# Loads of the first three tiles moved together ahead of the weights, and two fills moved from GpSimd to ScalarE, in an RWKV and two-expert-layer kernel

## The chip, the cores and the metric

The kernel runs on one core of a Trainium2 chip. The metric is the device time of one execution in microseconds (us): before the change 930.45 us is the median of three runs (929.73 to 933.15).

## The reference

Three layers follow one another. The first is a linear attention with a decaying state, for 4 batches, 8 heads, 768 steps and a head size of 48; its output, taken as 3072 tokens of 384 values, goes through a gated feed-forward layer (384 to 1536 and back), and this through a layer of eight experts in which each token goes to the expert with the largest logit.

```python
for t in range(S):                                   # attention, per batch and head
    cur = np.einsum('bhd,bhe->bhde', u[None] * kt, vt)
    y[:, :, t] = np.einsum('bhd,bhde->bhe', rt, state + cur)
    state = wt[:, :, :, None] * state + np.einsum('bhd,bhe->bhde', kt, vt)
xn = x / sqrt(mean(x * x) + 1e-6) * rms_g            # gated layer
x = (silu(xn @ w_gate) * (xn @ w_val)) @ w_out
e = argmax(x @ w_gate2)                              # experts, for each token
out = prob(e) * sigmoid(x @ w_output_gate)[e] * (relu(x @ w1[e]) @ w2[e])
```

The weights of the gated layer arrive as 64-bit floats; the others are 32-bit.

## The kernel before

**Tiles.** A tile is 128 steps of one batch; there are 24, numbered so that tiles 0 to 3 are the first 128 steps of the four batches. The gated layer works on blocks of three tiles; block 0 is tiles 0 to 2. While TensorE works on a block, the attention of the next block is laid in slots between its matmuls.

**Loads of a tile.** All go through the queue of SyncE (SP), which issues in program order. `load_tile` (L296) brings the transposed decays, k and r (the "set": two loads of 96 KB at L310 and two of 192 KB at L312, 576 KB together, into 48 of each 64 partitions), `load_rk` (L314) r and k with tokens on partitions (384 KB, L318, one buffer for all tiles) and `load_v` (L320) v (192 KB, L325). The padding rows of a set are filled by `pads` (L278): four fills and one of five columns; tile 2 has a set of its own in the ring, whose pads are on GpSimd (POOL, L303). Tiles 0 and 1 have theirs filled by VectorE and GpSimd.

**Weights of the gated layer.** They come in 18 pieces of 768 KB. Pieces 0, 1, 3 and 4 are the gate and value columns of one 128-wide slice f (two loads of 384 KB each), pieces 2 and 5 are rows of `w_out` for two slices (one load). `decode` (L101) turns the 64-bit words into two 32-bit parts in five stages: the loads; L113 on ScalarE and L114 on VectorE; L118 on VectorE and L122 on GpSimd; L125 on ScalarE; L130 on VectorE or GpSimd. One `decode_step` (L680) issues the loads of the piece two further on and takes earlier pieces on by a stage each.

**Attention of a tile** (`attention`, L339) is a generator with nine steps: (1) scan of the decays on VectorE, L357, and on GpSimd the products r*k*u, L363 and L364; (2) L367 and L368; (3) second scan L373, product L376, the loads of a later set, the sum over r*k*u on VectorE, L380, the loads of the next r and k, and L384 on GpSimd; (4) transposes and their copy, L391 and L393; (5) matmuls L403 and masks L407; (6) matmuls L420, sum L424, then on ScalarE and GpSimd the norm, L428 to L430; (7) matmuls L435, state copies L445, load of a later v; (8) L449; (9) transposes L453 and the two parts of x, L457 and L458.

**Start.** Before the first block the steps of tiles 0 to 2 are issued in the order of the tuple `START_SEQ` (L42): 0, 1 or 2 is the next step of that tile, 9 is a decode step, and a negative number is that many idle matmuls that warm TensorE (L332). Each engine runs its instructions in the order in which they are issued here. The first matmul of the gated layer (L165) needs x of tiles 0 to 2 and the first piece.

The loads in the order in which SP issues them: set 0, r and k of 0, v of 0, piece 0, set 1, piece 1, v of 1, piece 2, set 2, v of 2; then from the steps: set 3, r and k of 1, set 4, r and k of 2, v of 3, piece 3, r and k of 3, v of 4, pieces 4 and 5. `rk` has one buffer, so r and k of tile 1 are issued after L380 of tile 0, and those of tile 2 after L380 of tile 1:

```python
        nc.vector.tensor_reduce(g, rku, axis=AX.X, op=ALU.add)   # L380
        load_rk(i + 1)                                           # L381
```

The ring has 12 slots of 1536 words per partition and six larger ones; its first users are `kts`, two spare buffers, `turned` and v of tile 2, and then the decoded weights go round it. `states` (128x1536) is zeroed by GpSimd at L707.

Of the kernel before, what the change touches and what calls it, by code (L numbers as in the profile page):

```python
# [9 lines left out]
F32 = mybir.dt.float32  # L10
# [4 lines left out]
AF = mybir.ActivationFunctionType  # L15
# [7 lines left out]
def kernel(  # L23
# [15 lines left out]
    ROUTE_AT=(0, 1),  # L39
    OFFS=((0, 0, 6.7, 7.5, 8.8, 10.5, 11.4, 11.5, 12.7), (0, 1.6, 3.2, 4.8, 6.4, 8, 9.6, 11.6, 13.8)),  # L40
    TGAP=(8.9, 9.0),
    START_SEQ=(-11, 0, 0, 0, -4, -4, -6, -4, 0, 9, 1, 0, 1, -4, 0, 1, 1, 2, -4, 0, 0, 1, 9, 2, 0, 1, -4, 2, -6, 1, 9, 2, 1, 2, -4, 1, 2, 9, -2, 2, 2, 9, -6, 2, 9),  # L42
):
    nc = tc.nc
    B, S, _, H, D = rkv.shape
    N, DM = out.shape
    DFF = w_gate.shape[1]
    E, _, F2 = w1.shape
    P = 128
# [19 lines left out]
    SEG = P + 1  # L69
    FLAT = NPR * SEG  # L70
    KR = 2 * NPR * P
    SETW = KR + FLAT + 1
# [13 lines left out]
    def slot_of(n, dtype, name, big=None):  # L86

        if big is None:
            big = taken[0] % 3 == 2
            taken[0] += 1  # L90
        size = WSLOT if big else SLOT
        t = ring.tile([P, size], dtype, tag="big" if big else "ring", bufs=6 if big else 12, name=name)
        return t[:, 0:n]
# [75 lines left out]
    def ring_view(shape, dtype=F32, big=None):  # L169
        n = 1  # L170
        for x in shape:
            n *= x
        t = slot_of(n, dtype, "rv", big)
        names = "abc"[:len(shape)]
        dims = " ".join(names)
        return t.rearrange(f"p ({dims}) -> p {dims}", **dict(zip(names[1:], shape[1:])))
# [90 lines left out]
    p1 = ph1.enter_context(tc.tile_pool(name="p1", bufs=1))  # L267
# [8 lines left out]
    states = p1.tile([P, B, NPR, 2 * D], F32, name="states")  # L276

    def pads(t, engs):  # L278

        for q in range(2):  # L280
            engs[q].memset(t[64 * q + 32:64 * q + 64, KR:SETW], 1.0)
        for q in range(2):
            engs[q].memset(t[64 * q + 32:64 * q + 64, 0:KR], 0.0)
        engs[1].memset(t[:, KR:SETW:SEG], 0.0)

    def parts(t):

        kr = t[:, 0:KR].rearrange("p (x a t) -> p x a t", x=2, a=NPR)
        return kr, t[:, KR:SETW]

    tiles = [(b, ch) for ch in range(NCH) for b in range(B)]
    vt = {}
    rk = {}
    sets = {}

    def load_tile(i):  # L296

        if i >= len(tiles):
            return
        b, ch = tiles[i]  # L300
        if i == NSET:
            t = ring_view([SETW], big=True)
            pads(t, (nc.gpsimd, nc.gpsimd))  # L303
        else:
            t = sets_w[(i - (i > NSET)) % NSET]
        sets[i] = t
        kr, w = parts(t)
        w = w[:, 1:SETW - KR].rearrange("p (a t) -> p a t", t=SEG)[:, :, 0:P]
        for q in range(2):
            nc.sync.dma_start(out=w[64 * q:64 * q + D], in_=feat[b, ch, q, :, 0])  # L310
        for q in range(2):
            nc.sync.dma_start(out=kr[64 * q:64 * q + D], in_=feat[b, ch, q, :, 1:3])  # L312

    def load_rk(i):  # L314
        if i < len(tiles):
            b, ch = tiles[i]
            rk[i] = p1.tile([P, 2, H, D], F32, tag="rk", name="rk")
            nc.sync.dma_start(out=rk[i], in_=rkv[b, ch * P:ch * P + P, 0:2])  # L318

    def load_v(i):  # L320
        if i >= len(tiles):
            return
        b, ch = tiles[i]
        t = ring_view([H, D], big=False) if i == 2 else p3.tile([P, H, D], F32, tag="v", bufs=2, name="vt")
        nc.sync.dma_start(out=t, in_=rkv[b, ch * P:ch * P + P, 2])  # L325
        vt[i] = t
# [9 lines left out]

    START = START_SEQ

    def attention(c, i, xh, xl, col):  # L339
# [37 lines left out]
        if i != NSET:  # L377
            load_tile(i + NSET + (i < NSET))
        g = p2.tile([P, H], F32, tag="g", name="g")
        nc.vector.tensor_reduce(g, rku, axis=AX.X, op=ALU.add)  # L380
        load_rk(i + 1)  # L381
        vv = vt.pop(i)
        y = p2.tile([P, H, D], F32, tag="y", name="y")
# [235 lines left out]
    with tc.manual_schedule():  # L619
        one_b = const.tile([P, P], BF16, name="one_b")  # L620
        nc.vector.memset(one_b, 1.0)
        pads(sets_w[0], (nc.vector, nc.gpsimd))
        load_tile(0)
        c = constants()
        load_rk(0)
        load_v(0)
        pads(sets_w[1], (nc.vector, nc.gpsimd))
        kts = ring_view([NSET + 1, NPR * P], big=False).rearrange("p i (a t) -> p i a t", a=NPR)
        pieces = []
        for f in range(KF):  # L630
# [38 lines left out]
        def advance(m, stage):  # L669
            if m < len(pieces):  # L670
                while len(gens_w) <= m:
                    m0 = len(gens_w)
                    gens_w.append([decode(m0, *pieces[m0][:2], m0 % 3 == 2, *pieces[m0][2:]), 0])
                while gens_w[m][1] < stage:
                    next(gens_w[m][0])
                    gens_w[m][1] += 1
# [21 lines left out]

        turned = ring_view([4, KD * P], big=False)
        advance(0, 1)  # L700
        load_tile(1)
        advance(1, 1)
        load_v(1)
        advance(2, 1)
        load_tile(2)
        load_v(2)
        nc.gpsimd.memset(states, 0.0)  # L707

        xs = new_x(0)
        first = [attention(c, a, xs[0], xs[1], a * P) for a in range(sizes[0])]  # L710
# [32 lines left out]
        for j in range(NB):  # L743
# [24 lines left out]
            for f in range(KF + 2):  # L768
# [9 lines left out]
                if j == NB - 1:  # L778
                    if f >= 3:
                        next(xw, None)  # L780
                    if f == KF - 3:
                        xg0 = ring_view([EARLY // P, ROW])
                        nc.sync.dma_start(
                            out=xg0, in_=scr[0:EARLY, :].rearrange("(t p) c -> p t c", p=P)
# [253 lines left out]
        for ui, (k, r0, n) in enumerate(units):  # L1038
# [4 lines left out]
            a, b2 = ew[k]  # L1043
# [24 lines left out]
            for f in range(KF2 + 2):  # L1068
                if f < KF2:
                    o = bank("a", 2, [P, n])  # L1070
                    t = a[f // 2]
# [18 lines left out]
                if f >= 2:  # L1090
                    g = f - 2
                    hh, hl = hs.pop(g)
                    t = b2[g // 2]
# [36 lines left out]
        for q in ("w1", "w2"):  # L1130
            ov[q] = []
            for _ in range(2):
                t = slot_of(1536, F32, "ov")
# [57 lines left out]
```

## Time and profile before

| | before |
|---|---|
| median of three runs | 930.45 us (929.73 to 933.15) |
| the profiled execution | 934.85 us |
| its span, first to last instruction | 933.1 us |
| mean granted TensorE clock | 0.962 of full speed |
| busy: TensorE (PE) | 876.9 us, 94% |
| busy: VectorE (DVE) | 533.7 us, 57% |
| busy: ScalarE (ACT) | 314.8 us, 34% |
| busy: GpSimd (POOL) | 227.9 us, 24% |
| SP's load queue | 79.67 MB, 29.2% of 16 DMA engines' time |

The profile is one execution of the program. Its stretches differ: the start (attention of three tiles and the first decode steps), block 0 beside the rest of the decoding, and then blocks 1 to 7 and the experts, in which TensorE is hardly idle. Engines are named as in the profile: PE, DVE, ACT, POOL, and SPq for SP's queue. An idle time in brackets stands ahead of an instruction, with what ended it.

### The profile page before, as it was taken

The numbers are of one execution on the slowest core, as the hardware profiler recorded it, in microseconds if no ns is written. First come the engines' busy times: TensorE is split into PE (matmuls) and PEld (weight loads), VectorE is DVE, ScalarE is ACT, GpSimd is POOL, SyncE is SP. The second block draws the span as 40 slices with busy tenths as digits, with TensorE's granted clock in tenths as the row PEclk, the third lists the DMA queues.
The fourth block names the chain that finished last, engine by engine and source line by source line (L and its number), as shares of the span: only waits on it lengthen the run. The fifth ranks groups of instructions, "written<-read, shape, count | busy, mean of one in ns | idle before, by whom it ended". The sixth has DMA issues, their size and how long they took to land. (4 is left out here: it accounts for less than half of the span.)

```text
span 933.1 us, 14620 instructions
## 1 busy us (share of the span) xinstructions
PE 876.9 (94%) x5543; PEld 846.7 (91%) x5543; DVE 533.7 (57%) x1073; ACT 314.8 (34%) x654; POOL 227.9 (24%) x298
## 2 busy tenths in 40 slices
PE   6568779999999999999999999999899999999995
PEld 4458769999999999999999999999899999999994
DVE  5589785656565376366456465434537565556551
ACT  1254433322322323323222322323334344434430
POOL 6465552212231131132123113010010100122111
PEclk7679899999999999999999999999999999999997
DMA  9564252274131023022122122001143453554510
GB/s 229 129 218 131 90 161 50 83 213 137 46 110 51 9 86 82 13 78 56 47 69 60 52 68 78 1 27 51 52 146 98 151 179 107 159 163 152 174 47 21
DMA packets 65300, 90.40 MB, mean 97 GB/s; under 512 B 6259, under 2 KB 56035, under 8 KB 65229
## 3 DMA queue, kind: packets, MB, share of 16 engines
q1 hardware_dynamic: 60973, 79.67, 29.2%
q0 software_dynamic: 3568, 9.57, 2.8%
q8 instruction: 44, 0.72, 0.3%
q10 hardware_dynamic: 688, 0.22, 0.1%
q14 instruction: 27, 0.22, 0.1%
HBM read 73.22 MB, written 16.73 MB: 96 GB/s over the span
## 5 line engine op out<-in xcount | busy, mean ns | idle before, releaser
L165 PE MATMUL a<-xh,gv 128*128 128x384 f32 x1152 | 324.1, 347 | 0.0
L165 PEld LDWEIGHTS a<-xh,gv 128*128 128x128 f32 x1152 | 213.7, 191 | 2.2
L165 PE MATMUL a<-xl,gv 128*128 128x384 f32 x576 | 195.9, 340 | 0.0
L500 DVE TENSOR_TENSOR sil<-a,sil 128x384 f32<-128x384 f32 x96 | 53.2, 554 | 110.6 <-PE a L165 110.2
L165 PE MATMUL a<-xh,w1s 128*128 128x256 f32 (+7 forms) x432 | 111.9, 325 | 1.4 <-DVE hl L876 1.1
L165 PEld LDWEIGHTS a<-xl,gv 128*128 128x128 f32 x576 | 110.3, 192 | 0.0
L502 ACT ACTIVATE hh<-sil 128x384 fp32r<-128x384 f32 x96 | 50.3, 524 | 162.2 <-DVE sil L500 162.2
L514 PE MATMUL l<-wo,hh 128*128 128x400 f32 x288 | 102.2, 355 | 0.0
L498 ACT ACTIVATE sil<-a 128x384 f32<-128x384 f32 x96 | 47.2, 492 | 156.7 <-PE a L165 151.6
L515 PE MATMUL l<-wo,hh 128*128 128x400 f32 x288 | 99.8, 347 | 0.0
L516 PE MATMUL l<-wo,hl 128*128 128x400 f32 x288 | 99.2, 345 | 0.0
L244 POOL DMA_INDIRECT out_dram<-row,iu x30 | 34.9, 1165 | 208.5 <-DVE row L887 188.7
L876 DVE SCALAR_TENSOR_TENSOR hl<-a,hh 128x256 fp32r<-128x256 f32 (+7 forms) x80 | 40.7, 510 | 74.3 <-ACT hh L875 74.3
L165 PEld LDWEIGHTS a<-xh,w1s 128*128 128x128 f32 x432 | 76.7, 188 | 2.8 <-DVE hl L876 1.6
L505 DVE TENSOR_TENSOR hl<-sil,hh 128x384 fp32r<-128x384 f32 x96 | 56.2, 585 | 34.9 <-ACT hh L502 34.9
L875 ACT ACTIVATE hh<-a 128x256 fp32r<-128x256 f32 (+7 forms) x80 | 36.5, 456 | 101.9 <-PE a L165 100.2
L165 PE MATMUL a<-xl,w1s 128*128 128x256 f32 (+7 forms) x216 | 69.7, 323 | 0.1
L384 POOL TENSOR_TENSOR y<-vt,g 128x384 f32<-128x384 f32 x23 | 22.0, 958 | 169.2 <-issue 62.6
L165 PE MATMUL l<-rows,hh 128*128 128x384 f32 (+3 forms) x240 | 63.0, 344 | 0.0
L420 PE MATMUL m<-vt,am 128*128 128x48 f32 x368 | 55.1, 278 | 4.5 <-DVE am L407 4.5
L420 PEld LDWEIGHTS m<-vt,am 128*128 128x128 f32 x368 | 51.2, 204 | 5.5 <-DVE am L407 5.4
L514 PEld LDWEIGHTS l<-wo,hh 128*128 128x128 f32 x288 | 54.9, 190 | 0.1
(216 smaller groups left out, 1510.8 us busy)
## 6 DMA issues: line engine op xcount, KB each, us to landing
raw<-in_moe_w_dram SPq DMA_DIRECT2D x64, 384.0 KB, 3.3
rk<-in_rkv_dram SPq DMA_DIRECT2D x24, 384.0 KB, 4.2
set<-in_feat_dram SPq DMA_DIRECT2D x46, 192.0 KB, 3.9
scr<-zrow SPq DMA_DIRECT2D x8, 788.0 KB, 7.6
set<-in_feat_dram SPq DMA_DIRECT2D x46, 96.0 KB, 3.0
vt<-in_rkv_dram SPq DMA_DIRECT2D x23, 192.0 KB, 2.5
raw<-in_moe_w_gate_dram SPq DMA_DIRECT2D x8, 384.0 KB, 4.0
raw<-in_moe_w_val_dram SPq DMA_DIRECT2D x8, 384.0 KB, 3.9
```

The lines of the kernel that those rows point to most:

```text
L165: nc.tensor.matmul(o, a, b, start=start and i == 0, stop=stop and i == 2, skip_group_check=True)
L244: ins = nc.gpsimd.indirect_dma_start(out=dst, out_offset=bass.IndirectOffsetOnAxis(ap=idx, axis=0), in_=rows, in_offset=None, bounds_check ...
L420: nc.tensor.matmul(yp[:, 2 * p + q], am[q][:, p], vv[:, 2 * p + q], start=not ch, stop=True, skip_group_check=True,)
L498: nc.scalar.activation(out=sil, in_=o, func=AF.Silu)
L500: nc.vector.tensor_tensor(out=sil, in0=pg[1], in1=sil, op=ALU.mult)
L502: nc.scalar.activation(out=hh, in_=sil, func=AF.Copy)
L505: nc.vector.tensor_tensor(out=hl, in0=sil, in1=hh.bitcast(F32), op=ALU.subtract)
L514: nc.tensor.matmul(o, hh[:, sl], wh, start=f == 0, stop=False)
L515: nc.tensor.matmul(o, hh[:, sl], wl, start=False, stop=False)
L516: nc.tensor.matmul(o, hl[:, sl], wh, start=False, stop=f == KF - 1)
L875: nc.scalar.activation(out=hh, in_=o, func=AF.Relu)
L876: nc.vector.scalar_tensor_tensor(out=hl, in0=o, scalar=0.0, in1=hh.bitcast(F32), op0=ALU.max, op1=ALU.subtract)
```

## The change

The tuple moves one decode step (9) behind three steps of tiles 0 and 1 and four idle matmuls. Set 1, r and k of tile 1 and v of tile 1 are loaded ahead of piece 0, and set 2, r and k of tile 2 and v of tile 2 ahead of pieces 1 and 2. r and k of tiles 1 and 2 get a slot of the ring of their own (2 x 768 words). The four large fills of tile 2's pads, and that of `states`, are done by ScalarE, as an activation that copies a column of ones times 1 or 0. The fill of the five columns of tile 1's and tile 2's pads, and of tile 0's, is on GpSimd, as it was.

```diff
-    START_SEQ=(-11, 0, 0, 0, -4, -4, -6, -4, 0, 9, 1, 0, 1, -4, 0, 1, 1, 2, -4, 0, 0, 1, 9, 2, 0, 1, -4, 2, -6, 1, 9, 2, 1, 2, -4, 1, 2, 9, -2, 2, 2, 9, -6, 2, 9),
+    START_SEQ=(-11, 0, 0, 0, -4, -4, -6, -4, 0, 1, 0, 1, -4, 9, 0, 1, 1, 2, -4, 0, 0, 1, 9, 2, 0, 1, -4, 2, -6, 1, 9, 2, 1, 2, -4, 1, 2, 9, -2, 2, 2, 9, -6, 2, 9),
...
     def pads(t, engs):
-        for q in range(2):
-            engs[q].memset(t[64 * q + 32:64 * q + 64, KR:SETW], 1.0)
-        for q in range(2):
-            engs[q].memset(t[64 * q + 32:64 * q + 64, 0:KR], 0.0)
-        engs[1].memset(t[:, KR:SETW:SEG], 0.0)
+        for a, x in ((slice(KR, SETW), 1.0), (slice(0, KR), 0.0)):
+            for q in range(2):
+                rows = slice(64 * q + 32, 64 * q + 64)
+                if engs[q] is nc.scalar:
+                    nc.scalar.activation(
+                        out=t[rows, a], in_=one_b[rows, 0:1].to_broadcast([32, a.stop - a.start]),
+                        func=AF.Copy, scale=x,
+                    )
+                else:
+                    engs[q].memset(t[rows, a], x)
+        nc.gpsimd.memset(t[:, KR:SETW:SEG], 0.0)
...
             t = ring_view([SETW], big=True)
-            pads(t, (nc.gpsimd, nc.gpsimd))
+            pads(t, (nc.scalar, nc.scalar))
...
     def load_rk(i):
-        if i < len(tiles):
+        if i < len(tiles) and i not in sets_rk:
             b, ch = tiles[i]
-            rk[i] = p1.tile([P, 2, H, D], F32, tag="rk", name="rk")
+            sets_rk.add(i)
+            if i in (1, 2):
+                rk[i] = more_rk[:, i - 1].rearrange("p (x h d) -> p x h d", x=2, h=H)
+            else:
+                rk[i] = p1.tile([P, 2, H, D], F32, tag="rk", name="rk")
             nc.sync.dma_start(out=rk[i], in_=rkv[b, ch * P:ch * P + P, 0:2])
...
         pads(sets_w[1], (nc.vector, nc.gpsimd))
+        load_tile(1)
+        more_rk = ring_view([2, 2 * DM], big=False)
+        load_rk(1)
+        load_v(1)
         kts = ring_view([NSET + 1, NPR * P], big=False).rearrange("p i (a t) -> p i a t", a=NPR)
...
         advance(0, 1)
-        load_tile(1)
+        load_tile(2)
+        load_rk(2)
+        load_v(2)
         advance(1, 1)
-        load_v(1)
         advance(2, 1)
-        load_tile(2)
-        load_v(2)
-        nc.gpsimd.memset(states, 0.0)
+        flat = states.rearrange("p b a d -> p (b a d)")
+        nc.scalar.activation(
+            out=flat, in_=one_b[:, 0:1].to_broadcast(flat.shape), func=AF.Copy, scale=0.0
+        )
```

## Rows read from the trace of the kernel before

**Rows 1.** Stretches: us, then busy us (instructions) of each engine, clock, DMA share, GB/s.

```profile
3.00:9.50 6.50, 6.01 (x28) 2.87 (x26) 3.94 (x6) 0.55 (x1) 6.03 (x15) 1.00 0.96 254
9.50:14.40 4.90, 2.64 (x23) 1.37 (x20) 1.83 (x3) 0.60 (x1) 4.09 (x5) 0.77 1.11 228
14.40:18.80 4.40, 1.00 (x4) 0.91 (x5) 4.30 (x7) 0.91 (x1) 2.63 (x1) 0.50 1.08 337
...
23.30:31.40 8.10, 3.31 (x26) 2.94 (x24) 0.81 (x2) 0.12 (x1) 0.00 (x0) 0.71 0.90 193
31.40:62.70 31.30, 19.30 (x117) 15.41 (x118) 25.39 (x41) 15.13 (x30) 20.84 (x17) 0.72 0.51 166
62.70:150.00 87.30, 71.30 (x421) 67.72 (x422) 73.98 (x97) 41.01 (x79) 45.75 (x30) 0.88 0.38 119
150.00:900.00 750.00, 745.41 (x4783) 729.52 (x4782) 412.95 (x897) 250.69 (x532) 141.51 (x216) 1.00 0.30 89
```

**Rows 2.** Timeline of DVE in the start: start, us, instruction, idle before.

```profile
14.46 0.56 DVE L114 TENSOR_SCALAR dt<-raw 128x768 uint32<-128x768 uint32 x1 [1.03 <-DMA raw<-in_moe_w_val_dram]
...
33.51 0.55 DVE L380 TENSOR_REDUCE g<-rk 128x8 f32<-128x384 f32 x1 [9.36 <-POOL rk L364]
...
37.06 0.55 DVE L114 TENSOR_SCALAR dt<-rv 128x768 uint32<-128x768 uint32 x1
37.64 1.64 DVE L118 SCALAR_TENSOR_TENSOR dt<-rv,dt 128x768 uint32<-128x768 uint32 x1
...
47.47 0.94 DVE L118 SCALAR_TENSOR_TENSOR dt<-raw,dt 128x768 uint32<-128x768 uint32 x1
...
61.30 1.00 DVE L114 TENSOR_SCALAR dt<-rv 128x768 uint32<-128x768 uint32 x1
62.22 0.95 DVE L130 TENSOR_TENSOR gv<-dt,gv 128x768 fp32r<-128x768 f32 x1
```

**Rows 3.** Timeline of POOL in the start.

```profile
7.40 1.93 POOL L283 MEMSET rv<- 32x1024 f32 x2
...
9.43 1.39 POOL L707 MEMSET states<- 128x1536 f32 x1
10.77 1.00 POOL L363 TENSOR_TENSOR rk<-rk 128x384 f32<-128x384 f32 x1
...
16.15 2.63 POOL L122 TENSOR_TENSOR dt<-dt,raw 128x768 int32<-128x768 int32 x1 [1.81 <-DVE dt L118]
31.42 0.99 POOL L363 TENSOR_TENSOR rk<-rk 128x384 f32<-128x384 f32 x1 [12.63 <-DMA rk<-in_rkv_dram]
```

**Rows 4.** Timeline of SP's queue in the start: when a load was issued.

```profile
6.34 1.08 SPq L310 DMA_DIRECT2D set<-in_feat_dram  x2
...
24.33 0.35 SPq L318 DMA_DIRECT2D rk<-in_rkv_dram  x1
...
26.90 0.84 SPq L312 DMA_DIRECT2D set<-in_feat_dram  x2
34.09 0.35 SPq L318 DMA_DIRECT2D rk<-in_rkv_dram  x1
...
47.21 0.48 SPq L109 DMA_DIRECT2D rv<-in_moe_w_out_dram  x1
```

**Rows 5.** Waits of SP's queue, 0 to 60 us: total us, times, longest.

```profile
SPq L318 <- DVE g L380: 10.8, 2, 8.1
...
SPq L109 <- DMA raw<-in_moe_w_val_dram: 2.2, 1, 2.2
```

**Rows 6.** Single loads: r and k of tile 1, and piece 5, with us to landing.

```profile
rk<-in_rkv_dram SPq DMA_DIRECT2D x1, 384.0 KB, 7.0
...
rv<-in_moe_w_out_dram SPq DMA_DIRECT2D x1, 768.0 KB, 8.3
```

**Rows 7.** Timeline of ACT in the start.

```profile
9.76 0.60 ACT L393 ACTIVATE rv<-m 128x512 f32<-128x512 f32 x1 [6.21 <-PE m L391]
...
35.75 0.83 ACT L125 ACTIVATE gv<-dt 128x768 fp32r<-128x768 f32 x1
```

More of the change, by code (lines that the diff above doesn't have):

```diff
@@ L293 @@
     rk = {}
+    sets_rk = set()
     sets = {}
```

## The prediction, made before the changed kernel was timed

> **What bounds the kernel now.** I read the table of stretches first. From 150 to 900 us PE is busy for 745 of 750 us at full clock, so what starts earlier there ends earlier by as much; the change can only move what lies ahead. Ahead of it are a start of 62.7 us, in which no matmul of the gated layer runs, and block 0, where DVE (74 of 87.3 us) is busier than PE [rows 1]. In the start one stretch stands out: from 23.3 to 31.4 us every engine is nearly idle (DVE 0.81, ACT 0.12, POOL 0.00 us) while the DMA engines are 0.90 busy [rows 1].
>
> The timeline of DVE names the stop: the sum over r*k of tile 1 (L380) starts at 33.51 us after 9.36 us of idling for POOL's L364 [rows 2]. POOL's timeline goes one step back: L363 of tile 1 starts at 31.42, after 12.63 us of waiting for a load of r and k [rows 3]. SP's timeline goes back to the cause: that load was issued at 24.33, when sets, two weight pieces and piece 2 had gone before it, and it took 7.0 us to land behind them [rows 4, 6]. So this is a matter of the order of loads, and not of arithmetic. From 33.51 on DVE runs nearly without a gap to 62.22, the last split before the first block (25.39 us busy in the stretch from 31.4, whose first 2 us are idle) [rows 1, 2]: the start after the stop is DVE's.
>
> **How fast loads land.** Two rates bound every landing below. Before the first decode (L114 at 14.46, which had waited for the value columns) 576+384+192+768 = 1920 KB had landed from about 3 us on: 1920/11.4 = 168 KB/us [rows 1, 2]. By 31.3 (24.33+7.0), with r and k of tile 1, it was 5952 KB: 5952/28.3 = 210 KB/us [rows 4, 6]. The stretch from 14.4 to 18.8 reached 337 GB/s, so 210 is no ceiling [rows 1]. I take 210, as the mean over the longest stretch with the queue full, and 168 as the slow end.
>
> **The change part by part.**
> 1. *r and k of tile 1 early.* They are then the sixth part of the queue: 576+576 (sets 0 and 1)+384+192+384 = 2112 KB, landed by 3+2112/210 = 13.1 us (15.6 at 168). Set 1 is issued no earlier than the 6.34 us of now, as it waits for pads that stay where they are [rows 4]. POOL then does L363 and L364 of tile 1 in some 2.0 us, by about 17 at the latest, against 33.5. The stop at L380 is gone. What is late next is piece 0.
> 2. *Piece 0 later.* It now stands behind 2304 KB instead of 1152, so its 768 KB have landed at 3+3072/210 = 17.6 us (21.3 at 168), against 14.4. Queued behind L114 on DVE are, by the new tuple, the sum of tile 0 (L424) and the second scan of tile 1. The steps moved ahead of this decode step (scan and products of tile 1, masks of tile 0) fill DVE to about 15.5, so it idles some 2 us (6 at the slow end). From 17.6: L114 0.56, L118 0.95, L424 0.55, the scan 1.22, the product 0.69 give 21.6 for L380 of tile 1; I add 0.9 for POOL's product L122, which now runs beside the scan, and have 22.5. Gain at this point: 33.51-22.5 = 11.0 us [rows 2].
> 3. *Piece 1 later.* Set 2, r and k and v of tile 2 (1152 KB) go ahead of it: 4992 KB, landed at 26.8 us (32.7 at 168). DVE would want it 37.06-33.51 = 3.55 us after L380 [rows 2], at 26.05. So 0.7 of the 11.0 is lost: 10.3 (4.4 at the slow end).
> 4. *r and k of tile 2 early.* Their load waited for L380 of tile 1 until 34.09 (8.1 us, the longest of SP's waits of that kind) [rows 4, 5]; now they land by 3+4032/210 = 22.2. POOL's products of tile 2 then run ahead of the decode of piece 1 and not beside it: those loads were issued at 34.09, so the products fell beside L118 at 37.64, which took 1.64 us, against 0.94 for the same shape later [rows 2]. I count +0.7 for that, the bounds being 0 and 1.5 (both products). Gain 11.0.
> 5. *The same bytes behind.* Sets 3 and 4, v of 3, piece 3 and so on keep their order and shift forward by about 11 us, but the queue now has no gap at 31 us to catch up in. Piece 5 is the last that the start needs: 576x5+384x4+192x5+768x6 = 9984 KB, by 3+9984/210 = 50.5 us. It was issued at 47.21, landed 8.3 later, and DVE took it at 61.30 [rows 2, 4, 6]; after a shift by 11.0 it is wanted at 50.3. So the loads are just in time; I take off 1.0 us, with 0 (late loads are nearly all weights, the kind that flowed at 337 GB/s) and 4 (195 KB/us, landing at 54.3) as bounds. Gain 10.0.
> 6. *Fills by ACT.* Rows for 128x512 and 128x768 (0.60 and 0.83 us) give 0.9 ns an element, so 2x517, 2x1024 and 1536 elements cost 0.6+0.6+1.05+1.05+1.5 = 4.8 us, an estimate from these two rows [rows 7]. ACT is idle for 6.21 us before L393 at 9.76 [rows 7], which covers it. Nothing on the path; without the cover it would be up to 1.5 us for L393, and nobody waits for that within 5 us. POOL is rid of 1.93 and 1.39 us of fills and some smaller ones, and starts on tile 0's products up to 1.9 us earlier than 10.77 [rows 3], which piece 0's arrival swallows: counted at nothing. POOL's small fill of five columns now waits for ACT's fills of ones, 1.2 us after ACT comes free at 3.55 (its 0.55 from 3.0 [rows 1]), and POOL has fills of its own until past 6: nothing. Set 2's loads wait for the same fills, done by about 7; SP reaches them after piece 0, later than that. Two more notes on SP: it stops for an earlier load at times (w_out behind the value columns, 2.2 us [rows 5]), which paces it and doesn't empty the queue, and r and k of tiles 1 and 2 no longer make it wait for L380 [rows 5].
>
> In the row POOL was the loser where the two met: L122 of piece 0 took 2.63 us beside DVE's scan, which kept its length [rows 3]. Hence the 0.9 in point 2 and not more. The Trainium skill (SBUF — State Buffer, section SBUF: two separate sides) has it that GpSimd and a two-input VectorE operation take a shared port pair by an exclusive lock, and whichever starts first holds it for the whole instruction. By that rule the scan of tile 1 would wait out L122 and point 2 would lose about 1.9 instead of 0.9, the sum being 9.0; this case's L118 beside L363 (1.64 us) agrees with it, the scan beside L122 doesn't.
>
> **The sum.** 10.0 us of the start, kept through block 0 (whose loads wait for buffers and not for the queue) and the full PE after it. 934.85-10.0 = 924.9 for an execution like the profiled one, which lies 0.47% above the median; against the median of 930.45 that is **920.5 us**.
>
> **The rivals.**
> - *The forecast, a shift by 7 to 13.5 us* (917 to 923.5 us: 7 from point 5's 4; 13.5 with point 2's 0.9, point 3's 0.7, point 4's 0.8 more and point 5's 1.0 given back). For it: an idle stretch on all engines with one named releaser. 0.73.
> - *Part of it, 4.7 to 7 us* (923.5 to 925.8): piece 5 lands 4 to 6.3 us after it is wanted, which is the queue at 195 to 186 KB/us. For it: set 0 is in the first 168 KB/us, and three sets now come first. 0.10.
> - *No change:* the loads bind all through the start. At 168 KB/us piece 5 lands at 3+9984/168 = 62.4 us, which is when it was used before (61.30) [rows 2]: 930 to 932. Against it: 210 over the full queue, 337 in one stretch. With it goes the case that the change doesn't do what it says (L363 of tile 1 still waits, because r and k of both tiles share one tile and the first product waits for the second load; then only some 2 us go, as that load lands by 22). 0.12.
> - *Slower, by the clock:* in block 0 the mean granted clock is 0.88 over 87.3 us [rows 1], so with two levels of 0.5 and 1 PE spent 0.24x87.3 = 21 us at 1.2 GHz. The clock was at 0.50 from 14.4 to 18.8 us, after a stretch in which PE had worked for 2.64 of 4.9 [rows 1]. If pieces come later to block 0 and PE idles between them, that share grows, and each microsecond at the low level costs up to half of one. It decides where the low time goes past 21+2x(10.0+4.7) = 50 us; at 60 us the cost is 19.5, less the 10.0: 940 us. Against it: the stretch 31.4 to 62.7 already has 0.72 before block 0 [rows 1], and the loads there are asked for by decode steps, not by the start. 0.05. The Trainium skill (TensorE: Matmul & The Clock Gate, section What's actually happening) says that the throttled state is the default and activity lifts it; the row from 14.4 agrees, and no row shows a block 0 with later pieces.
>
> **How the numbers follow.** The number is that of the likeliest case. The range goes from 916.5 (a gain of 13.5 and a little scatter) to 926 (the second case in whole); above it lie the last two cases, 0.17. About 0.5% (4.65 us) is what a measurement here can tell from no change, so faster means under 925.8: the first two cases, 0.83; same 0.12; slower 0.05.
>
> **What would show it right or wrong.** L363 of tile 1 starting by 17 us; DVE's idle time before L380 of tile 1 gone, and in its place 1 to 4 us before the first L114; that L114 at 17 to 19; L380 of tile 1 at 21 to 24; the first L165 at 51 to 54 instead of 62.7; ACT's five fills done before 9 us; the stretch after the start with the same busy times and a clock near 0.88. The prediction is wrong if the first L114 is after 21, if new DMA waits of over 3 us in all stand before L113 or L114 of pieces 2 to 5, or if block 0 grows by more than 3 us.

## The result and the profile after

| | before | after |
|---|---|---|
| median, timed side by side | 931.03 us (929.73 to 933.15, 4 runs) | 922.59 us (921.59 to 923.18, 4 runs) |
| ratio, with its 95% interval | | 0.9907 [0.9894, 0.992] |
| the profiled execution | 934.85 us | 922.08 us |
| its span | 933.1 us | 920.4 us |
| mean granted TensorE clock | 0.962 | 0.970 |

The change saves 8.4 us (0.93%) where 10.0 and a time of 920.5 us had been forecast, inside the range of 916.5 to 926. Between the two profiled executions it is 12.8 us (12.7 between their spans), and both numbers matter below.

The stretches of the changed kernel (columns as in [rows 1]) have no idle one left: the 8.1 us of the kernel before in which DVE, ACT and POOL nearly stood still [rows 1] are gone. From 22.2 us to the first matmul of the gated layer DVE is busy for 24.63 of 28.70 us; the stretch behind it (87.3 us from the first matmul of block 0) has the same busy times and nearly the same clock as before, and the full-PE part is the same.

```profile
8.50:17.00 8.50, 6.36 (x36) 4.75 (x35) 6.74 (x10) 0.69 (x3) 7.09 (x5) 0.69 1.09 279
17.00:22.20 5.20, 5.03 (x23) 4.20 (x22) 5.08 (x6) 1.92 (x4) 3.44 (x3) 0.52 1.05 319
22.20:50.90 28.70, 21.61 (x133) 17.21 (x134) 24.63 (x42) 15.23 (x30) 17.98 (x14) 0.79 0.79 230
50.90:60.90 10.00, 9.39 (x36) 8.88 (x37) 9.37 (x11) 4.88 (x9) 6.89 (x4) 0.57 0.47 156
...
50.90:138.20 87.30, 72.11 (x419) 68.05 (x420) 74.34 (x98) 40.65 (x79) 46.78 (x30) 0.87 0.39 120
138.20:888.00 749.80, 745.20 (x4789) 729.32 (x4788) 412.95 (x898) 251.07 (x532) 141.32 (x218) 1.00 0.29 89
```

SP's timeline (start, us, load) answers to [rows 4]: r and k of tile 1 go out at 8.06 instead of 24.33, those of tile 2 at 13.42 instead of 34.09, and piece 5 at 34.67 instead of 47.21.

```profile
8.06 0.42 SPq L329 DMA_DIRECT2D rv<-in_rkv_dram  x1
...
13.42 0.35 SPq L329 DMA_DIRECT2D rv<-in_rkv_dram  x1
...
34.67 0.44 SPq L109 DMA_DIRECT2D rv<-in_moe_w_out_dram  x1
```

POOL's timeline answers to [rows 3] (the product of r and k is L374 now). Tile 1's starts at 14.53 with no wait, where it had waited 12.63 us and started at 31.42.

```profile
9.01 1.80 POOL L374 TENSOR_TENSOR rk<-rk 128x384 f32<-128x384 f32 x1 [2.75 <-DMA vt<-in_rkv_dram]
...
14.53 0.99 POOL L374 TENSOR_TENSOR rv<-rv 128x384 f32<-128x384 f32 x1
...
18.59 1.83 POOL L122 TENSOR_TENSOR dt<-dt,raw 128x768 int32<-128x768 int32 x1 [1.66 <-DVE dt L118]
...
25.50 1.00 POOL L375 TENSOR_TENSOR rv<-rv,u_bc 128x384 f32<-128x384 f32 x1
```

DVE's timeline answers to [rows 2]: L391 is the sum over r*k (L380 before). The 9.36 us of idling are gone; what is left is 0.84 us for piece 0 ahead of the first L114. Two of the instructions shown take longer than others of the same shape: the scan L384 (2.54 us; the scans of the other tiles take 1.22) and L114 of piece 1 (1.23; 0.55 in [rows 2]).

```profile
16.91 0.56 DVE L114 TENSOR_SCALAR dt<-raw 128x768 uint32<-128x768 uint32 x1 [0.84 <-DMA raw<-in_moe_w_val_dram]
...
18.98 2.54 DVE L384 TENSOR_TENSOR_SCAN rq<-set,front 128x516 f32<-128x516 f32 x1
...
22.16 0.54 DVE L391 TENSOR_REDUCE g<-rv 128x8 f32<-128x384 f32 x1
...
25.70 1.23 DVE L114 TENSOR_SCALAR dt<-rv 128x768 uint32<-128x768 uint32 x1
26.95 0.96 DVE L118 SCALAR_TENSOR_TENSOR dt<-rv,dt 128x768 uint32<-128x768 uint32 x1
...
49.49 0.63 DVE L114 TENSOR_SCALAR dt<-rv 128x768 uint32<-128x768 uint32 x1
50.04 0.95 DVE L130 TENSOR_TENSOR gv<-dt,gv 128x768 fp32r<-128x768 f32 x1
```

ACT's timeline answers to [rows 7]: the five fills take 3.43 and 1.48 us and are over at 8.50, ahead of L404 (L393 before).

```profile
3.56 3.43 ACT L284 ACTIVATE rv<-one_b 32x517 f32<-32x517 bf16 x4
7.02 1.48 ACT L722 ACTIVATE states<-one_b 128x1536 f32<-128x1536 bf16 x1
9.70 0.60 ACT L404 ACTIVATE rv<-m 128x512 f32<-128x512 f32 x1 [1.20 <-PE m L402]
```

Last the first matmul of the gated layer, in PE's timeline, of the kernel before and of the changed one:

```profile
62.73 0.67 PE L165 MATMUL a<-xh,gv 128*128 128x384 f32 x1
```

```profile
50.92 0.67 PE L165 MATMUL a<-xh,gv 128*128 128x384 f32 x1
```

It comes 11.81 us earlier. The copies at the end of block 0 start at 159.61 instead of 171.09, 11.48 us earlier, and those at the end of each later block, down to block 7 (657.18 instead of 668.66), by the same 11.48. The last 1.2 us of the 12.7 between the spans come behind block 7.

### The profile page after: what moved, and what is told of

It is laid out like the page before. It is cut to its first block, busy times and chain, and to the rows that moved or that the text cites. A ratio compares the mean times of both kernels' runs of the same rounds, so it can differ in the third digit from the quotient of the medians.

```text
span 920.4 us, 14623 instructions
## 1 busy us (share of the span) xinstructions
PE 878.3 (95%) x5543; PEld 847.3 (92%) x5543; DVE 534.9 (58%) x1073; ACT 319.5 (35%) x659; POOL 226.2 (25%) x293
## 5 line engine op out<-in xcount | busy, mean ns | idle before, releaser
L516 DVE TENSOR_TENSOR hl<-sil,hh 128x384 fp32r<-128x384 f32 x96 | 58.1, 605 | 34.9 <-ACT hh L513 34.9
L527 PEld LDWEIGHTS l<-wo,hl 128*128 128x128 f32 x288 | 55.1, 191 | 0.2
```

The costliest lines, as they stand in the source:

```text
L516: nc.vector.tensor_tensor(out=hl, in0=sil, in1=hh.bitcast(F32), op=ALU.subtract)
L527: nc.tensor.matmul(o, hl[:, sl], wh, start=False, stop=f == KF - 1)
```

## The experiments

Each kernel has one profiled execution, the kernel before has three and the changed one two. All but the two repeats of the kernel before were also timed against the kernel before on the same chip, whose medians there were 931.03 to 931.97 us. "Sum 1" is the start of the sum over r*k of tile 1, "first matmul" that of the gated layer in the profiled execution.

| kernel | median us | ratio to before [95%] | sum 1 | first matmul |
|---|---|---|---|---|
| before, three profiles | | | 33.51, 31.93, 30.19 | 62.73, 61.62, 59.89 |
| after | 922.59 | 0.9907 [0.9894, 0.992] | 22.16 | 50.92 |
| after, again | 924.1 | 0.9913 [0.9896, 0.993] | 22.14 | 51.10 |
| r and k early only | 923.37 | 0.9913 [0.9893, 0.9932] | 23.44 | 54.06 |
| all but r and k early | 931.95 | 1.0009 [0.9997, 1.0022] | 29.04 | 59.84 |
| fills on GpSimd | 923.84 | 0.9913 [0.9894, 0.9932] | 22.68 | 52.03 |
| old order of steps | 926.63 | 0.9955 [0.9939, 0.997] | 26.22 | 54.69 |
| r and k of tile 2 late | 925.3 | 0.9931 [0.9915, 0.9946] | 22.05 | 54.40 |
| scan ahead of the decode | 925.43 | 0.9937 [0.9919, 0.9954] | 18.23 | 52.03 |
| old sequence of loads | 924.35 | 0.9923 [0.9906, 0.9939] | 23.45 | 52.65 |
| piece 0 behind set 1 | 922.66 | 0.9913 [0.9896, 0.993] | 21.85 | 50.74 |

A profiled execution need not be a middle one: with r and k early only it was the slowest of six (926.01 us), with the old order of steps the fastest of seven (925.47). So the last column, which is one execution each, and the medians do not rank these kernels alike.

**The kernel before, a second and a third profile.** No edit.

> The kernel before, unchanged, for a second profile. Question: the two profiled executions differ by 12.7 us, the medians by 8.4. If the start of the kernel before varies (the load of r and k of tile 1 landing earlier or later), the first matmul of the gated layer comes at 58 to 60.5 us here and not at 62.7, and the sum over r*k of tile 1 at 29 to 31.5 and not at 33.5. If the start is fixed and what varies lies behind it, the two stand at 62.7 and 33.5 within 0.5 us, and the span differs in block 0 or among the experts.

> The kernel before, unchanged, a third profile. The first two had the sum over r*k of tile 1 at 33.51 and 31.93 us, the first matmul of the gated layer at 62.73 and 61.62, and 264.4 and 263.1 us from the end of block 7 on; their times (934.85 and 932.5) lie above the median of 931.1. If the landing of r and k of tile 1 varies from run to run, the sum comes at another time again, and block 0 and blocks 1 to 7 keep their length within 0.5 us; what comes behind block 7 is 263.1 or 264.4 by the clock. If the start is fixed, the sum is at 31.9 or 33.5 again.

POOL's timeline, product of r and k of tile 1, in the second profile and then in the third:

```profile
29.84 0.99 POOL L363 TENSOR_TENSOR rk<-rk 128x384 f32<-128x384 f32 x1 [11.67 <-DMA rk<-in_rkv_dram]
```

```profile
28.09 0.99 POOL L363 TENSOR_TENSOR rk<-rk 128x384 f32<-128x384 f32 x1 [9.90 <-DMA rk<-in_rkv_dram]
```

The start of the kernel before is not fixed: r and k of tile 1 are there at 31.42 [rows 3], 29.84 or 28.09 us, and sum 1 shifts by the same amounts. Most of that reaches the first matmul (1.11 of 1.58 us in the second profile, 2.84 of 3.33 in the third), and what lies between it and the end of block 7 keeps its length: from the first matmul to the end of block 0 it is 108.36, 108.48 and 108.68 us in the three, from there to the end of block 7 497.57 in each. The execution that the prediction was made against has the latest of the three landings. The 58 to 60.5 expected for the second profile was missed (61.62), the third one met it (59.89). The second and the third were taken on different chips, so whether the landing varies with the execution or with the chip is not separated.

**r and k of tiles 1 and 2 early, and nothing else.** On the kernel before:

```diff
+            if i in (1, 2):
+                rk[i] = more_rk[:, i - 1].rearrange("p (x h d) -> p x h d", x=2, h=H)
+            else:
+                rk[i] = p1.tile([P, 2, H, D], F32, tag="rk", name="rk")
...
+        more_rk = ring_view([2, 2 * DM], big=False)
...
         load_tile(1)
+        load_rk(1)
         advance(1, 1)
...
         load_tile(2)
+        load_rk(2)
         load_v(2)
```

> The kernel before, with r and k of tiles 1 and 2 in the ring and loaded behind the set of their own tile; weights, sets, fills and the order of the steps stay as they were. Theory (the stop was r and k landing late): the sum over r*k of tile 1 starts at 24 to 25 us instead of 33.5, the scan of tile 2 may then wait some 2 us for set 2 (which 384 KB more stand ahead of), and 6 to 8 us are gained: 923 to 925 us, ratio 0.991 to 0.994. Rival 1 (the sets ahead of the weights and the moved decode step bring the gain): under 3 us, 928 or more. Rival 2 (the lighter GpSimd brings it): under 2 us.

Two loads moved give 0.9913, which can't be told from the whole change. POOL's product of tile 1 starts without a wait, and DVE's sum 1 at 23.44; this kernel's lines are POOL's and then DVE's. Its first matmul at 54.06 belongs to the slowest of its six runs, so it does not say that the rest of the change is worth 3 us:

```profile
18.13 1.44 POOL L368 TENSOR_TENSOR rv<-rv 128x384 f32<-128x384 f32 x1
```

```profile
23.44 0.55 DVE L385 TENSOR_REDUCE g<-rv 128x8 f32<-128x384 f32 x1
```

**All but that.** The changed kernel, with r and k of tiles 1 and 2 in the one buffer and loaded from the steps:

```diff
-            if i in (1, 2):
-                rk[i] = more_rk[:, i - 1].rearrange("p (x h d) -> p x h d", x=2, h=H)
-            else:
+            if True:
...
-        load_rk(1)
         load_v(1)
...
-        load_rk(2)
         load_v(2)
```

> The changed kernel, but r and k of tiles 1 and 2 stay in the one buffer and are loaded when the tile before has been summed, as in the kernel before; sets and v come ahead of the weights, the decode step stays moved, the fills are by ScalarE. Theory: SP reaches the load of r and k of tile 1 behind set 3 at about 20 us, it lands at 26 to 28, the sum over r*k of tile 1 starts at 28.5 to 30.5, that of tile 2 waits again; 2 to 5 us gained of the 8.4: 926 to 929 us. Rival 1 (order of sets and steps): 6 to 9 us gained, 922 to 925. If it is slower than the kernel before, sets ahead of weights cost by themselves.

No gain: 1.0009 [0.9997, 1.0022], less than the 2 to 5 us of the theory and far from the 6 to 9 of the rival. Sum 1 does come earlier (29.04) than in the three profiles of the kernel before. But on POOL the decode product of piece 0 (L122), which runs in the shadow of the wait in the kernel before (16.15 in [rows 3]), is queued behind the late products, and the scan of tile 2 on DVE then meets it:

```profile
26.95 0.99 POOL L372 TENSOR_TENSOR rk<-rk 128x384 f32<-128x384 f32 x1 [12.88 <-DMA rk<-in_rkv_dram]
...
28.97 1.82 POOL L122 TENSOR_TENSOR dt<-dt,raw 128x768 int32<-128x768 int32 x1
```

```profile
29.04 0.55 DVE L389 TENSOR_REDUCE g<-rk 128x8 f32<-128x384 f32 x1 [9.71 <-POOL rk L373]
29.51 2.37 DVE L366 TENSOR_TENSOR_SCAN kq<-rv,back 128x516 f32<-128x516 f32 x1
```

The scan takes 2.37 us instead of 1.22, and the decode of piece 1 (L114) comes at 33.74, where the third profile of the kernel before has it at 33.73: the 1.15 us by which sum 1 is earlier than there are the 1.15 us by which the scan is longer.

**The fills back on GpSimd.**

```diff
-            pads(t, (nc.scalar, nc.scalar))
+            pads(t, (nc.gpsimd, nc.gpsimd))
...
-        flat = states.rearrange("p b a d -> p (b a d)")
-        nc.scalar.activation(
-            out=flat, in_=one_b[:, 0:1].to_broadcast(flat.shape), func=AF.Copy, scale=0.0
-        )
+        nc.gpsimd.memset(states, 0.0)
```

> The changed kernel with the fills of tile 2's pads and of the states on GpSimd again. Theory: the product of r and k of tile 0 starts at 10.7 instead of 9.0, the sum of tile 0 0.6 us later, and the wait of the first decode for piece 0 (0.84 us) takes that up; first matmul of the gated layer within 0.5 us of the changed kernel's 50.9, time 922 to 923.5. Rival 2 (GpSimd relief matters): 2 us or more slower than the changed kernel, 925 or more.

The median is 923.84, and the ratio (0.9913) can't be told from that of the changed kernel. In the profiled execution sum 1 is 0.5 us and the first matmul 0.9 to 1.1 us later than in the two profiles of the changed kernel, more than the 0.5 expected. So the fills are worth about 1 us at the first matmul by this one profile, and no gain that the times can show.

**The old order of steps.**

```diff
-    START_SEQ=(-11, 0, 0, 0, -4, -4, -6, -4, 0, 1, 0, 1, -4, 9, 0, 1, 1, 2, -4, 0, 0, 1, 9, 2, 0, 1, -4, 2, -6, 1, 9, 2, 1, 2, -4, 1, 2, 9, -2, 2, 2, 9, -6, 2, 9),
+    START_SEQ=(-11, 0, 0, 0, -4, -4, -6, -4, 0, 9, 1, 0, 1, -4, 0, 1, 1, 2, -4, 0, 0, 1, 9, 2, 0, 1, -4, 2, -6, 1, 9, 2, 1, 2, -4, 1, 2, 9, -2, 2, 2, 9, -6, 2, 9),
```

> The changed kernel with the old order of steps: the first decode step stands again ahead of the scan and products of tile 1 and the masks of tile 0. Theory: VectorE stops at 12.8 us for piece 0, which lands at 16.9, and the 3.4 us of steps that were moved ahead of it now come behind it; sum over r*k of tile 1 at 24 to 25.5 instead of 22.2, 1.5 to 3.5 us slower than the changed kernel: 924 to 926 us. Rival (piece 0's place in the queue alone sets this, the order of steps does not matter): within 0.7 us of the changed kernel.

Here DVE stands 4.10 us for piece 0, and then 2.39 us for the matmuls of tile 0, whose masks now come behind the decode. DVE's timeline:

```profile
16.62 0.56 DVE L114 TENSOR_SCALAR dt<-raw 128x768 uint32<-128x768 uint32 x1 [4.10 <-DMA raw<-in_moe_w_val_dram]
...
23.88 0.56 DVE L435 TENSOR_TENSOR y<-m,y 128x384 f32<-128x384 f32 x1 [2.39 <-PE m L431]
...
26.22 0.54 DVE L391 TENSOR_REDUCE g<-rv 128x8 f32<-128x384 f32 x1
```

Sum 1 is 4.1 us later than in the changed kernel and the first matmul 3.6 to 3.8; the median is 926.63. The theory holds in its direction and fell short in size (sum 1 by 25.5 at the latest and 924 to 926 us had been expected); the wait of 2.39 us for the matmuls was not in it. With the sets ahead of piece 0 the moved decode step is needed.

**r and k of tile 2 late.**

```diff
-            if i in (1, 2):
+            if i == 1:
...
         load_tile(2)
-        load_rk(2)
         load_v(2)
```

> The changed kernel with r and k of tile 2 alone loaded late again, behind the sum of tile 1, in the old buffer. Theory: the load is issued at about 26 us behind sets 3 and 4, lands at 30 to 32; GpSimd's products of tile 2 end at 32 to 34 and the decode product of piece 1 (28.05 in the changed kernel) waits behind them on GpSimd until then, so the second part of piece 1 and the norm of tile 1 come 4 us later; VectorE loses 1 to 3 us: first matmul of the gated layer at 52 to 54, 923.5 to 926 us. Rival (only the first stop mattered): within 0.7 us of the changed kernel. The prediction put 0.7 on this part.

The stop comes back one tile later. POOL's timeline, then DVE's:

```profile
32.43 1.00 POOL L374 TENSOR_TENSOR rk<-rk 128x384 f32<-128x384 f32 x1 [8.07 <-DMA rk<-in_rkv_dram]
...
34.46 1.82 POOL L122 TENSOR_TENSOR dt<-dt,rv 128x768 int32<-128x768 int32 x1
```

```profile
34.53 0.55 DVE L391 TENSOR_REDUCE g<-rk 128x8 f32<-128x384 f32 x1 [2.58 <-POOL rk L375]
```

The first matmul at 54.40 lies just outside the 52 to 54 expected, the median of 925.3 inside the 923.5 to 926. By these profiles r and k of tile 2 are worth 3.3 to 3.5 us at the first matmul, where the prediction had put 0.7 on that part. By the medians it is 2.2 us (925.3 against 923.1 over all runs of the changed kernel), and the intervals of the ratios just overlap.

**The second scan ahead of the decode**, to spare the 0.84 us and the long scan:

```diff
-    START_SEQ=(-11, 0, 0, 0, -4, -4, -6, -4, 0, 1, 0, 1, -4, 9, 0, 1, 1, 2, -4, 0, 0, 1, 9, 2, 0, 1, -4, 2, -6, 1, 9, 2, 1, 2, -4, 1, 2, 9, -2, 2, 2, 9, -6, 2, 9),
+    START_SEQ=(-11, 0, 0, 0, -4, -4, -6, -4, 0, 1, 0, 1, -4, 1, 9, 0, 1, 2, -4, 0, 0, 1, 9, 2, 0, 1, -4, 2, -6, 1, 9, 2, 1, 2, -4, 1, 2, 9, -2, 2, 2, 9, -6, 2, 9),
```

> The changed kernel with the third step of tile 1 (second scan, product, sum over r*k) put ahead of the first decode step. In the changed kernel VectorE idled 0.84 us for piece 0 ahead of that decode step, and the scan behind it took 2.54 us beside GpSimd's product of piece 0 against 1.22 us alone. Theory (the scan was blocked by GpSimd): scan back to 1.2 us, no idle time ahead of the decode, 1 to 2 us faster: first matmul of the gated layer at 49 to 50, 920.5 to 921.7 us. Rival (the decode of piece 0 is what the rest waits for): no change or up to 1 us slower.

A miss. Sum 1 came 3.9 us earlier, and yet the first matmul 1.1 us later. The moved scan met the other product of POOL (L375), and the next scan met L122. DVE's timeline, then POOL's:

```profile
15.57 2.02 DVE L384 TENSOR_TENSOR_SCAN rq<-set,front 128x516 f32<-128x516 f32 x1
...
18.23 0.54 DVE L391 TENSOR_REDUCE g<-rv 128x8 f32<-128x384 f32 x1
...
21.14 2.67 DVE L368 TENSOR_TENSOR_SCAN kq<-rv,back 128x516 f32<-128x516 f32 x1
```

```profile
15.17 1.33 POOL L375 TENSOR_TENSOR rv<-rv,u_bc 128x384 f32<-128x384 f32 x1
...
20.88 1.84 POOL L122 TENSOR_TENSOR dt<-dt,raw 128x768 int32<-128x768 int32 x1 [0.95 <-DVE dt L118]
```

What it saved at the one scan it paid at the next, and L114 of piece 1 is at 26.39 instead of 25.70. Later DVE waits 1.44 us for eight matmuls (L446), which take 1.67 us here at a granted clock of 0.50 (32.9 to 34.6 us) and 0.94 in the changed kernel at 1.00 (32.2 to 33.2). The median of 925.43 is 2.3 us above that of the changed kernel, beyond the 1 us of the rival; what the times add to the 1.1 us at the first matmul is not explained.

**The changed kernel again, and two other sequences of loads.** The first has no edit. The second puts set 1 and set 2 back behind the pieces, with r and k behind their sets; the third loads piece 0 between set 1 and r and k of tile 1.

```diff
-        load_tile(1)
         more_rk = ring_view([2, 2 * DM], big=False)
-        load_rk(1)
-        load_v(1)
...
         advance(0, 1)
+        load_tile(1)
+        load_rk(1)
+        advance(1, 1)
+        load_v(1)
+        advance(2, 1)
         load_tile(2)
         load_rk(2)
         load_v(2)
-        advance(1, 1)
-        advance(2, 1)
```

```diff
         load_tile(1)
         more_rk = ring_view([2, 2 * DM], big=False)
-        load_rk(1)
-        load_v(1)
...
         advance(0, 1)
+        load_rk(1)
+        load_v(1)
         load_tile(2)
```

> The changed kernel once more, beside the two below on one chip. Theory: it waits for no late load of r and k, so its start is steadier than that of the kernel before: first matmul of the gated layer at 50.5 to 51.5, median 921.8 to 923.3, ratio 0.990 to 0.992.

> The changed kernel with the old sequence of sets and pieces (piece 0 ahead of set 1, pieces 1 and 2 ahead of set 2), r and k of tiles 1 and 2 behind their sets; the fills on ScalarE and the new order of steps stay. Theory (r and k early is nearly the whole gain, the order of sets and pieces nearly nothing): VectorE waits some 2 us for set 1 at the scan of tile 1 and no longer for pieces 0 and 1; the sum over r*k of tile 1 at 22.5 to 24, first matmul of the gated layer at 51 to 53, 922.5 to 924.5 us. Rival (sets ahead of the weights are needed): as the kernel with r and k alone, or slower, 925 or more.

> The changed kernel with piece 0 loaded between set 1 and r and k of tile 1. Theory: piece 0 lands by about 14.5 us, so the first decode has no 0.84 us of waiting, r and k of tile 1 land by 16 and their products are done ahead of the sum; first matmul of the gated layer 0 to 0.9 us earlier, 921.5 to 922.8. Rival (what stands behind the first decode on GpSimd, and the clock, decide): no gain or up to 1.5 us slower.

The start of the changed kernel is the same in its two profiles: sum 1 at 22.16 and 22.14, first matmul at 50.92 and 51.10. Its median the second time was 924.1, above the 921.8 to 923.3 expected, with a ratio of 0.9913 within the 0.990 to 0.992. All its ten runs go from 921.59 to 925.48 with a median of 923.1. Its times are no steadier for the steadier start: on the chip of the second timing they spread over 3.8 us (six runs), those of the kernel before over 4.2 (eleven). The other two lie where they were expected (924.35 and 922.66), though VectorE's wait for set 1 is 0.99 us where 2 had been expected, and the wait of 0.84 us that the third spares at piece 0 moves sum 1 by only 0.3 us (21.85). None of these sequences of loads, all with r and k early and the new order of steps, can be told from another by these intervals, and no version was found that beats the changed kernel.

## Why the prediction was right

**The stop and its cause.** Right. Leaving out the early r and k leaves out the whole gain (1.0009), and doing them alone gives it nearly whole (0.9913). The order of sets and pieces, the moved decode step and the fills bring nothing between them that these times can show; the moved decode step only pays for the later piece 0.

**Point 1 and point 2.** L363 of tile 1 had to start by 17 and started at 14.53. The first L114 came at 16.91 (17.6 forecast), after 0.84 us of idling and not 2, as DVE reached it at 16.07. Sum 1: 22.16 (22.5), the earlier L114 giving 0.7 and the longer scan taking 0.4 of it back, as the 0.9 for POOL beside the scan was 1.3 (2.54 less 1.22).

**Here the reading of the row failed.** I had taken from L122's 2.63 us [rows 3] that POOL is the loser where the two meet. What decides is who starts first. In the kernel before the scan had started 0.2 us ahead of L122 (16.15), as DVE's timeline shows:

```profile
15.94 1.23 DVE L357 TENSOR_TENSOR_SCAN kq<-set,back 128x516 f32<-128x516 f32 x1
```

In the changed kernel L122 started at 18.59 and the scan at 18.98, and the scan ended 1.1 us after L122. In the scans of 2.37, 2.02 and 2.67 us above POOL had started first too, and each ended 1.1 us after POOL's product. The Trainium skill (SBUF — State Buffer, section SBUF: two separate sides) has this as its rule: whichever of the two starts first holds the shared port pair for its whole instruction. The trace agrees with it, and so does the row that I had called a disagreement. The price in point 2 was still not the 1.9 that I had put beside the rule but 1.3, because L122 was already under way.

**Point 3.** Wrong in its cause, right in its size by luck. No DMA wait stood before L114 of piece 1; the queue was faster than the 210 KB/us that I took (279 and 319 GB/s in the stretches to 22.2). But that L114 took 1.23 us instead of 0.55, beside POOL's L375 at 25.50, so 0.7 went all the same. Where r and k of tile 2 were late and POOL did not run beside it, the same L114 took 0.55 (at 25.59).

**Point 4.** Under-sized. L118 of piece 1 took 0.96 instead of 1.64 us, the 0.7 that was counted, but DVE's product of tile 2 behind it (L368, L379 in the changed kernel) came down by another 0.7, so that 1.4 were gained, near the upper bound of 1.5. The product in DVE's timeline, of the kernel before and of the changed one:

```profile
39.29 1.39 DVE L368 TENSOR_TENSOR kq<-rv,kq 128x512 f32<-128x512 f32 x1
```

```profile
27.92 0.66 DVE L379 TENSOR_TENSOR kq<-rv,kq 128x512 f32<-128x512 f32 x1
```

What was missed besides is that POOL's products of tile 2 stand ahead of other work on POOL's queue: left late in the changed kernel, they cost 3.3 to 3.5 us at the first matmul.

**Point 5.** Piece 5 was taken at 49.49 with no wait: the 1.0 us was not lost. The gain at the first matmul is 11.81 against the execution that the sum was made for, where 10.0 had been forecast: 1.0 more here, 0.7 more in point 4 and 0.35 more in point 2, less 0.3 that went when a sum of DVE (L435 at 39.85) waited 0.39 us for its matmuls.

**Point 6.** The fills cost ACT 3.43+1.48 = 4.9 us (4.8 estimated) and were over at 8.50. Their worth, counted as nothing, is about 1 us at the first matmul by one profile, and not to be seen in the times.

**Why the median gained less than the profiled execution.** The durations came from one execution, and that was a late one: its wait for r and k was the longest of three profiles. In the three the profiled time less the first matmul's start is 872.1, 870.9 and 871.0 us; by their mean, 871.3, the median of 931.03 has its first matmul at about 59.7 (an estimate), and from there to 51.0 it is 8.7 us, about the 8.4 that were measured. So carrying the sum over to the median, as if every run had the wait of the profiled one, was too large by about 3.0 us (62.73 less 59.7), and the sum itself was too small by 1.8. That 10.0 came as near to 8.4 as it did is in part luck: the two errors go against each other.

**The signs.** Three of those named came out just outside their bounds: DVE idled 0.84 us before the first L114 (1 to 4), that L114 started at 16.91 (17 to 19), and the first matmul came at 50.92 (51 to 54). The others came as they were named.

**The rivals.** "Part of it" and "no change", both by late loads, fell: piece 5 was taken with no wait. So did the case of a shared tile: the product of tile 1 started at 14.53, 1.1 us after the load of tile 2's r and k was issued (13.42), and the four loads of r and k in the first 60 us of the kernel before took 3.1 to 7.0 us to land. The clock in block 0 is real but small. In 12 of the 13 profiles of these kernels block 0 lasts 108.05 to 109.10 us; in the second profile of the changed kernel it lasts 111.87, with the clock lower for 20 us in a row (stretches of that profile, then of the first):

```profile
111.10:121.10 10.00, 8.25 (x36) 7.59 (x34) 9.97 (x14) 3.16 (x5) 4.93 (x4) 0.55 0.80 212
121.10:131.10 10.00, 10.00 (x48) 9.98 (x49) 3.87 (x9) 2.80 (x7) 4.37 (x4) 0.60 0.29 96
```

```profile
110.92:120.92 10.00, 8.40 (x52) 7.85 (x51) 9.96 (x14) 3.04 (x5) 4.19 (x3) 0.84 0.66 177
120.92:130.92 10.00, 7.02 (x49) 6.41 (x48) 7.15 (x15) 5.90 (x14) 6.42 (x5) 1.00 0.30 101
```

That is 3.2 us more than in the first profile, over the 3 us of growth at which the prediction called itself wrong. The same program has both, so these profiles do not show it as an effect of the change; whether the earlier start makes it more frequent was not tried.

## What to carry to other kernels

When every engine idles while the load queue is full, ask which load the idle chain waits for and what stands ahead of it; here two loads of 384 KB moved forward were worth as much as the whole reordering. An early load must not push a needed one back, and where it does, the step that needs the other has to move too (3.6 to 3.8 us at the first matmul here). Before a gain is carried from one profiled execution to the median, take a second and a third profile: here a wait for a load behind a full queue differed by 3.3 us among three of them.

## What the runs showed of the hardware

- A late landing is not a fixed number: under the same full queue r and k of tile 1 were used at 31.42, 29.84 and 28.09 us. With the loads early, sum 1 was the same within 0.02 us in two profiles.
- GpSimd and VectorE block each other by order of start. When POOL's product had started first, a scan of 1.22 us took 2.02 to 2.67 in the lines shown and ended 1.1 us after it; when the scan had started first, the product L122 took 2.63 instead of 1.83. It goes for an operation with a single source too: L114 (128x768) took 1.23 us instead of 0.55 when L375 had started 0.2 us ahead of it.
- Behind block 7 the profiles fall into two groups, 263.1 to 263.3 and 264.3 to 264.5 us to the end, for the same program too (264.4 and 263.1 of the kernel before). PE idles there in the routing (1.15 and 1.75 us before two of its matmuls), and in the first profile the matmuls after it go on at the lower clock for some 3 us longer than in the second: granted clock 0.50 and then 0.69 in the two stretches of 4 us from 674.66, against 0.57 and 1.00 from 673.67. The same nine matmuls of the experts' first layer, in PE's timeline of the first profile of the kernel before and of the second:

```profile
679.18 2.11 PE L165 MATMUL a<-rv,w1s 128*128 128x256 f32 x9
```

```profile
677.83 1.23 PE L165 MATMUL a<-rv,w1s 128*128 128x256 f32 x9
```

This accounts for 1.2 us of the 12.7 between the two profiled spans; as one program shows both, it is not shown to come from the change.
